# The last eight pieces of the second weights are converted beside the first transform, under new order tables

## The chip, the core and the metric

The kernel runs on one core of a Trainium2 chip. The metric is device time in microseconds (us) of that core for one execution. Three timed runs of the kernel before gave 977.62, 979.89 and 982.78 us. The profile comes from one more execution, of 984.61 us, whose span from the first to the last instruction is 982.6 us.

The core has five instruction streams. PE multiplies matrices (its weight loads are listed as PEld), DVE is the vector engine, ACT the scalar engine, POOL the GpSimd engine, and SP issues all transfers, those that transpose 16-bit data too.

## The reference

Two stages follow each other, for 4 sequences of 768 tokens.

Attention has 8 heads of width 64. Each query and key is assigned to the nearest of 16 centroids, and a query sees only keys of its own cluster:

```
mask   = q_assign[:, :, :, None] == k_assign[:, :, None, :]
scores = where(mask, scale * q @ k.T, -1e9)
out    = softmax(scores) @ v
```

The heads are laid side by side (width 512), and a feed-forward layer with a Fourier mix follows:

```
X  = fft(fft(x, axis=1), axis=2)
u  = x + real(X)
un = (u - mean(u)) / sqrt(var(u) + 1e-6)
y  = u + relu(un @ w_ch1) @ w_ch2        # w_ch1 512x2048, w_ch2 2048x512
```

All is float32. The kernel reaches that precision with pairs of float16 numbers, a high and a low part, and three products for each multiplication.

## The kernel before

The work is cut into streams that are written as generators. A plan (`Overlap.PLAN`, a string) says in which order their steps are traced; a second set of tables (`Order.TABLE`, one string for each engine) then lists the order in which each engine's instructions stand. Nothing is decided at run time: every engine works through its own list, and waits by semaphore where an operand or a buffer is not ready. The streams are:

- `p0` to `p15`, preparation of a pair of heads (four pairs to a sequence): load q and k, find the largest value (L395), scale and split into high and low (L413 on ACT, L414 on DVE), assign clusters (L446 to L481).
- `s0` to `s15`, scores: for each of six blocks of 128 queries 12 matmuls for both heads of the pair (L509) and 4 for the mask (L514), one pass on DVE for each head that finds the row's limit (L528), the exponential on ACT (L530), high and low part of it (L542 on ACT or L540 on POOL, L543 on POOL), and a transposing transfer (L545).
- `u1`, `u3`: for some early heads the transposition is done on PE instead (L562).
- `a0` to `a15`, products with v (18 matmuls for a block and head, L595 to L597, or 6 in float32, L590) and the division (L605 to L609), which writes into `X`, one 128x6x512 tile for a sequence; two such tiles take turns.
- `l` and `w`, loads and conversion of the weights. The 32 pieces (128x512 float32 each, 16 of either matrix) lie in an arena of 48 KB for each partition. `signs` takes the top bits (L698, L699 on ACT), `block` finds the largest over a group of pieces by 16 matmuls at L710 and a reduction (L714) with four tiny operations (L58 to L63), `join` rebuilds the number in PSUM (L725 on PE, L728 on DVE), `halve` writes the high part (L734 on ACT) and the low part (L740 on DVE for even pieces; L737 on ACT and L738 on POOL for odd ones). `relative` (L778 to L782) needs all pieces.
- `t0` to `t3`, the transform of a sequence: tables are loaded into the arena (L898), `fold` adds and subtracts mirrored rows and columns on DVE (L856, L857), splits (L839, L840) and transposes by transfer (L863), then come matmuls (L917, L933), three thirds with tables of their own (L906), and the sums into `X` (L983 to L992).
- `n0` to `n3`, the normalisation of the three blocks of a sequence (L1026 to L1054); the normalised rows are transposed by transfer (L1040).
- `f0` to `f3`, the two matrix products of a sequence: 576 matmuls up (L1069) and 288 down (L1111), with evictions at L1074 to L1078 and L1115.

The weights and the transform share the arena. Pieces take turns at four places (`EARLY`, at byte 0, 8224, 20576 and 28800, two pieces of 4112 bytes at each); the sign bits lie at 16448, 37024 and 41120, and a float32 copy at 45216 (`X32`). The transform's tables and folds begin at byte 20576, so with `LATE = 0` they overlap places that the weights use until the last piece is done. The class already knows a second layout for the last `2 * LATE` pieces: `place` puts them at `SPARE` (byte 0 and 8224), their sign bits at 16448, and the float32 copy over the piece itself, all below byte 20576; they are grouped by two instead of four.

PSUM has three buffers for everything but scores and outputs (`ps_f`): weights, transforms, preparation and the feed-forward products take turns in them.

Of the kernel before, what the change touches and what calls it, by code (L numbers as in the profile page):

```python
# [90 lines left out]
.2 -8 .2 9 -5 4 0 -6 5 .2 -8 0 7 -2 1 .4 3 -4 0 3 -4 1 1 .4 2 0 -4 3 .3 -7 6 .14 3 0 -5 4 .2 2 .2 -12 11 1 5 0 -21 11 1 .2 7
0 -20 10 8 -9 8 0 -6 5 -23 23 -2 1 0 -13 12 .3 -16 16 1 -4 1 1 0 2 1 4 0 -11 0 1 1 2 4 -3 -6 7 0 -4 3 0 -11 10 .4 2 -3 0 6 -6
.3 2 .2 -5 4 .2 1 -2 1 .12 7 0 -9 11 -12 12 -2 -12 0 11 -12 0 13 -14 13 -12 11 0 -13 0 4 .2 4 .3 6 0 -8 7 0 -5 4 0 -11 10 .2
13 -14 0 -15 14 .2 9 0 -11 -18 17 .3 -21 20 .2 3 3 1 -6 5 0 -7 6 .6 -13 12 .3 -15 14 .9 1 .2 6 -11 3 .2 4 0 -5 0 -3 5 0 3 1 1
# [1144 lines left out]
```

## Time and profile before

| | |
|---|---|
| timed runs | 977.62, 979.89, 982.78 us |
| profiled execution | 984.61 us, span 982.6 us |
| mean granted clock of PE | 0.984 of full speed |
| busy, of the span | PE 93%, DVE 60%, ACT 59%, POOL 59% |
| first conversion of a high half (L734) | 34.9 us |
| last one | 189.6 us |
| first matmul up (L1069) | 238.8 us |
| start of the last sequence's products, which then stand alone | 853.70 us |

Read the page's second part, 40 slices, for the stretches: PE is busy for 70 to 90% of most slices in the first quarter of the span, and for 90% or more of nearly every slice behind it, while DVE is busy for 80 to 90% of most slices of that first quarter. A share over the whole span hides both.

### The profile page before, as it was taken

What the parts mean: (1) busy time and instruction counts of PE and PEld (TensorE: products, weight loads), DVE (VectorE), ACT (ScalarE), POOL (GpSimd) and SP (SyncE); (2) the same over time, 40 slices, a digit from 0 to 9 for tenths busy, and PEclk for the clock granted to TensorE, in tenths of its full rate; (3) what the DMA queues carried; (4) which work ended last, traced back from release to release, by engine and by line L of the source; (5) the groups of instructions that cost most, each with busy time, mean ns of one, the idle gap of its engine ahead of it and who ended that gap; (6) DMA issues with size and microseconds to landing.
All of it is one profiled execution on the core that took longest, in us unless ns stands there. A gap on an engine that the chain in (4) does not pass through costs nothing.

```text
span 982.6 us, 23428 instructions
## 1 busy us (share of the span) xinstructions
PE 910.7 (93%) x9352; PEld 610.6 (62%) x9369; DVE 587.4 (60%) x1334; ACT 579.2 (59%) x924; POOL 577.7 (59%) x691
## 2 busy tenths in 40 slices
PE   2779979778999999999999999999999999999998
PEld 0347747645747657576757667567567485676583
DVE  6889899888656565678654655786463334511010
ACT  6687789557737747548756466568475472433140
POOL 2681862557967746748975658469766472553140
PEclk9989999979999999999999999999999999999999
DMA  7995894589868697598994768797684663311000
GB/s 268 200 263 138 204 258 111 125 149 184 140 146 148 110 172 149 112 180 165 138 192 89 145 122 155 137 184 142 112 135 81 121 122 65 74 24 34 11 12 22
DMA packets 359741, 131.21 MB, mean 134 GB/s; under 512 B 344272, under 2 KB 345296, under 8 KB 359632
## 3 DMA queue, kind: packets, MB, share of 16 engines
q1 hardware_dynamic: 359632, 129.72, 65.9%
q8 instruction: 73, 1.20, 0.5%
q14 instruction: 36, 0.29, 0.1%
HBM read 43.17 MB, written 6.29 MB: 50 GB/s over the span
## 4 chain that ended last, share of the span: by engine, by line
PE 46%; DMA 17%; DVE 11%; ACT 10%; POOL 8%; issue 5%; SPq 2%; POOLq 0%; ACTq 0%; DVEq 0%
PE ps_f L1069 15%; PE ps_f L1111 15%; DMA pt<-ph 14%; PE ps_big L509 5%; POOL ph L543 4%; ACT ph L542 3%; PE ps_o L590 2%; PE ps_f L917 2%; PE ps_f L562 2%; DVE arena L856 2%; ACT p L530 1%; DVE ps_big L528 1%; DVE amx L395 1%; PE ps_big L514 1%; POOL arena L1078 1%
## 5 line engine op out<-in xcount | busy, mean ns | idle before, releaser
L543 POOL TENSOR_TENSOR ph<-p,ph 128x768 f16<-128x768 f32 x144 | 241.9, 1682 | 148.1 <-ACT ph L542 120.9
L1069 PE MATMUL ps_f<-arena,w1h 128*128 128x256 f16 x1536 | 266.2, 274 | 4.8 <-DVE ps_big L528 2.3
L1111 PE MATMUL ps_f<-w2h,arena 128*128 128x512 f16 x768 | 236.8, 380 | 0.0
L1069 PE MATMUL ps_f<-arena,w1l 128*128 128x256 f16 x768 | 210.3, 274 | 0.0
L528 DVE TENSOR_SCALAR_CACHE_REDUCE ps_big<-ps_big,sce 128x768 f32<-128x768 f32 x144 | 142.5, 1021 | 91.6 <-PE ps_big L514 85.2
L1111 PEld LDWEIGHTS <-arena 128*128 128x128 f16 x1152 | 110.3, 98 | 127.5 <-issue 2.7
L530 ACT ACTIVATE p<-ps_big,rmx 128x768 f32<-128x768 f32 x144 | 129.3, 898 | 86.5 <-DVE ps_big L528 61.7
L1078 POOL TENSOR_TENSOR arena<-arena 128x256 f16<-128x256 f32 x192 | 130.3, 687 | 74.9 <-ACT arena L1077 71.6
L1069 PEld LDWEIGHTS <-w1h 128*128 128x128 f16 x1536 | 150.5, 98 | 26.1 <-issue 5.6
L542 ACT CAST ph<-p 128x768 f16<-128x768 f32 x144 | 119.8, 832 | 67.4 <-DMA pt<-ph 65.8
L1111 PE MATMUL ps_f<-w2l,arena 128*128 128x512 f16 x384 | 145.7, 379 | 0.0
L509 PE MATMUL ps_big<-hlk,hlq 64*128 64x384 f16 x1152 | 117.8, 333 | 8.3 <-ACT p L530 6.3
L595 PE MATMUL ps_o<-v,pt 128*128 128x66 f16 x1008 | 104.5, 194 | 17.9 <-DMA pt<-ph 17.4
L1074 DVE TENSOR_SCALAR arena<-ps_f,wrel 128x256 f32<-128x256 f32 x96 | 46.2, 481 | 118.0 <-PE ps_f L1069 79.3
L1077 ACT ACTIVATE arena<-ps_f,wrel 128x256 f16<-128x256 f32 x192 | 88.6, 473 | 44.3 <-DVE arena L1074 44.2
L595 PEld LDWEIGHTS <-pt 128*128 128x128 f16 x1008 | 92.6, 97 | 30.2 <-DMA pt<-ph 21.8
L596 PE MATMUL ps_o<-v,pt 128*128 128x64 f16 x1008 | 104.3, 195 | 0.0
L597 PE MATMUL ps_o<-v,pt 128*128 128x66 f16 x1008 | 103.9, 193 | 0.0
L596 PEld LDWEIGHTS <-pt 128*128 128x128 f16 x1008 | 92.9, 97 | 2.6
L597 PEld LDWEIGHTS <-pt 128*128 128x128 f16 x1008 | 93.2, 99 | 0.0
L509 PEld LDWEIGHTS <-hlq 64*128 64x128 f16 x1152 | 51.2, 96 | 59.1 <-issue 32.4
L1069 PEld LDWEIGHTS <-w1l 128*128 128x128 f16 x768 | 75.3, 98 | 11.5 <-issue 2.5
(187 smaller groups left out, 1356.7 us busy)
## 6 DMA issues: line engine op xcount, KB each, us to landing
arena<-in_moe_w_ch_dram SPq DMA_DIRECT2D x32, 512.0 KB, 5.2
scr<-in_q_dram SPq DMA_DIRECT2D x16, 384.0 KB, 3.8
vst<-in_v_dram SPq DMA_DIRECT2D x16, 384.0 KB, 4.0
scr<-in_k_dram SPq DMA_DIRECT2D x16, 384.0 KB, 4.4
out_dram<-arena SPq DMA_DIRECT2D x24, 256.0 KB, 2.3
pt<-ph SPq DMA_TRANSPOSE x156, 3.9
arena<-in_cs_dram SPq DMA_DIRECT2D x12, 192.0 KB, 4.4
arena<-in_ss_dram SPq DMA_DIRECT2D x12, 192.0 KB, 4.3
```

Of the source, the lines that this page charges most:

```text
L509: nc.tensor.matmul(out=ps[j][:, hf, 0:SH], lhsT=hq[rows[j], a, sl], rhs=hk[rows[j], c, hs], start=(i == 0), stop=False)
L528: nc.vector.tensor_scalar(out=ju, in0=ps[j][:, :, 0:SH], scalar1=ne, scalar2=None, op0=ALU.mult, op1=ALU.min, accum_out=m)
L530: nc.scalar.activation(x, ju, AF.Exp, bias=m, scale=-1.0)
L542: nc.scalar.copy(out=ph[:, 0], in_=p32)
L543: nc.gpsimd.tensor_tensor(out=ph[:, 1], in0=p32, in1=ph[:, 0], op=ALU.subtract)
L595: nc.tensor.matmul(out=o[:, at:at + W], lhsT=hi, rhs=v16[:, kt, 0:W], start=(kt == 0), stop=False)
L596: nc.tensor.matmul(out=o[:, at:at + D], lhsT=hi, rhs=v16[:, kt, 66:130], start=False, stop=False)
L597: nc.tensor.matmul(out=o[:, at:at + W], lhsT=lo, rhs=v16[:, kt, 0:W], start=False, stop=(kt == ST - 1))
L1069: nc.tensor.matmul(out=ps.rearrange("p (t x) -> p t x", x=P), lhsT=a[:, dc, fs], rhs=c[:, :, dc], start=(i == 0), stop=(i == 11))
L1077: nc.scalar.activation(hh[:, f], ps, AF.Relu, scale=rel[:, f:f + 1])
L1078: nc.gpsimd.tensor_tensor(out=hl[:, f], in0=r, in1=hh[:, f], op=ALU.subtract)
L1111: nc.tensor.matmul(out=ps, lhsT=a[:, f, ts], rhs=c[:, f], start=(i == 0), stop=(i == 47))
```

## The change

`LATE` goes from 0 to 4, so the last eight pieces of `w_ch2` (pieces 24 to 31) use the second layout, and their four groups have two pieces each: ten groups in all, not eight. The plan and the order tables are replaced as a whole.

```diff
     ID, TOP, MX, ONE = 47360, 47872, 47936, 48064
-    LATE = 0
+    LATE = 4
...
     PLAN = """
-p0 v0 c p0*2 p1 p0 p1 p0*2 c l p0*5 p1 w p2 l*3 p0 p2 l*3 w*2 p1 v1 p1*4 s0*3 w p2 w*4 p1*2 w*2 s0*2 p1 v2 w v3 s0*6 w*2 p2*2
+v0 c w p0*8 l v0 l*2 w p1*3 c p0*3 v0 p0 p2 p1 l*2 s0*2 v1 s0 a0 p1*4 w*4 v2 w*2 p1 w s0 w*2 a0 l*3 p1*2 l*3 s0 w*2 a0*2 w*2
...
     TABLE = {
         "PE": """
-.6 2 -3 2 0 -4 3 .2 1 -2 42 -39 0 -5 4 46 0 -53 4 47 -48 47 -54 7 0 -4 3 43 -44 0 -6 5 0 40 0 -41 -2 1 0 38 -39 39 -39 -2 1 0
+.5 3 0 -5 4 0 -6 5 .2 1 0 -11 12 -6 5 0 1 -7 10 0 -12 3 2 -2 1 4 -5 4 -3 2 3 -4 5 -6 0 1 0 9 -9 8 -9 8 -9 8 -9 .3 13 -14 4 0
...
```

In the kernel after, the lines that follow the tables have numbers larger by two (L856 is L858 there); the text uses the numbers of before, and only the rows below show the others.

DVE, around the first transform's fold (L856), before: the last two joins of the weights (L728) stand ahead of the fold, the last low half (L740) behind it.

```order
L609 TENSOR_TENSOR X_63<-ps_o,rs 128x3x128
L728 SCALAR_TENSOR_TENSOR ps_f<-arena,ps_f 128x512 x2
L856 TENSOR_TENSOR arena<-X_63 128x1536
L740 SCALAR_TENSOR_TENSOR w2l<-ps_f,wsc,w2h 128x512
L460 TENSOR_REDUCE mx<-ps_f 128x24
L528 TENSOR_SCALAR ps_big,rmx<-ps_big,sce 128x2x384
L462 TENSOR_TENSOR ac<-ps_f,mx 128x384
L528 TENSOR_SCALAR ps_big,rmx<-ps_big,sce 128x2x384
L395 TENSOR_REDUCE amx<-scr 128x1 x2
L395 TENSOR_REDUCE amx<-vst 128x1
L840 SCALAR_TENSOR_TENSOR arena<-arena,vseq 128x768
```

The same place after (`winv` and `wsc` are the scales of a group of pieces, `X_63` the tile of the first sequence).

```order
L611 TENSOR_TENSOR X_63<-ps_o,rs 128x3x128
L730 SCALAR_TENSOR_TENSOR ps_f<-arena,ps_f 128x512
L858 TENSOR_TENSOR arena<-X_63 128x1536
L742 SCALAR_TENSOR_TENSOR w2l<-ps_f,wsc,w2h 128x512
L397 TENSOR_REDUCE amx<-scr 128x1
L530 TENSOR_SCALAR ps_big,rmx<-ps_big,sce 128x2x384 x2
L842 SCALAR_TENSOR_TENSOR arena<-arena,vseq 128x768
L716 TENSOR_REDUCE arena<-ps_f 128x1
L858 TENSOR_TENSOR arena<-X_63 128x1536
L58 TENSOR_SCALAR ps_f<-arena 128x1
L397 TENSOR_REDUCE amx<-scr 128x1
L859 TENSOR_TENSOR arena<-arena 128x3x255
```

The fold now stands behind the first of the late groups, and the other three groups (each with a reduction like L716 and its tiny operations) stand between the transform's own instructions.

POOL at the same place before: two low halves of softmax rows (L543) and one of the weights (L738) stand ahead of the transform's second fold step (L857), which needs the fold.

```order
L543 TENSOR_TENSOR ph<-p_2706,ph 128x768
L868 TENSOR_TENSOR arena<-arena,X_63 1x255
L543 TENSOR_TENSOR ph<-p_2744,ph 128x768
L738 TENSOR_TENSOR w2l<-arena,w2h 128x512
L857 TENSOR_TENSOR arena<-arena 128x3x255
```

After, the same stretch:

```order
L483 COPY oh<-oh 128x12x16
L481 TENSOR_SCALAR oh<-oh 128x12x16
L368 MEMSET v_2975 128x6x2
L870 TENSOR_TENSOR arena<-arena,X_63 1x255
L859 TENSOR_TENSOR arena<-arena 128x3x255
L740 TENSOR_TENSOR w2l<-arena,w2h 128x512
L545 TENSOR_TENSOR ph<-p_2446,ph 128x768
L545 TENSOR_TENSOR ph<-p_2455,ph 128x768
```

The low halves now stand behind the second fold step.

POOL ahead of the first normalisation's subtraction (L1039), which the first matmul up needs, before: one softmax low half (L543) stands in the last six rows.

```order
L991 TENSOR_TENSOR X_63<-X_63,arena 128x257
L543 TENSOR_TENSOR ph<-p_3033,ph 128x768
L1048 TENSOR_TENSOR rest<-mv,mhalf 128x2
L992 TENSOR_TENSOR X_63<-X_63,arena 128x255
L1049 TENSOR_TENSOR rt<-rest 128x2
L1039 TENSOR_TENSOR arena<-arena 128x512
```

After:

```order
L740 TENSOR_TENSOR w2l<-arena,w2h 128x512
L993 TENSOR_TENSOR X_63<-X_63,arena 128x257
L994 TENSOR_TENSOR X_63<-X_63,arena 128x255
L545 TENSOR_TENSOR ph<-p_3031,ph 128x768
L1050 TENSOR_TENSOR rest<-mv,mhalf 128x2
L545 TENSOR_TENSOR ph<-p_3074,ph 128x768
L1041 TENSOR_TENSOR arena<-arena 128x512
```

The subtraction now stands behind two low halves, and behind the first two sums of the transform's last third.

Counted over the lists, these stand ahead of the first matmul up on PE: 32 blocks of scores before, 30 after; three products of 18 matmuls fewer; all weights and the whole first transform in both. On DVE, ahead of its first eviction of that product (L1074), there are 64 passes of L528 before and 60 after, 14 of L414 and 12, 8 groups of L714 with L58 to L63 and 10. After the last product of attention and ahead of the last transform's first matmul, PE has 48 matmuls of L1111 before, and 180 of L1069 and 60 of L1111 after.

## Rows read from the trace of the kernel before

**Rows 1.** The page's first part: busy us (share of the span) xinstructions.

```profile
PE 910.7 (93%) x9352; PEld 610.6 (62%) x9369; DVE 587.4 (60%) x1334; ACT 579.2 (59%) x924; POOL 577.7 (59%) x691
```

**Rows 2.** Busy time of each engine in three stretches of the span.

```profile
core 0: us, PE busy (x) PEld busy (x) DVE busy (x) ACT busy (x) POOL busy (x), PEclk, DMA share, GB/s
189.60:238.75 49.15, 32.93 (x404) 22.35 (x401) 41.65 (x90) 30.21 (x49) 29.05 (x30) 0.86 0.84 152
...
28.00:189.60 161.60, 141.22 (x1510) 96.44 (x1527) 144.55 (x325) 127.13 (x175) 92.69 (x94) 0.96 0.81 189
...
238.75:853.70 614.95, 602.58 (x6546) 404.06 (x6547) 362.63 (x815) 369.27 (x603) 406.50 (x459) 1.00 0.73 135
```

**Rows 3.** The chain of waits near its end: start us, us, what.

```profile
816.28 10.37 PE ps_f L1111 x48
...
853.70 20.96 PE ps_f L1069 x192
...
958.02 20.73 PE ps_f L1111 x96
```

**Rows 4.** One line each: counts, duration ns min/median/max, first and last start.

```profile
L734 ACT ACTIVATE w2h<-ps_f,wsc x16: 671/680/697, 127.0 to 189.6; 128x512 f16<-128x512 f32 x16
```

**Rows 5.** Groups of DVE from 189.6 to 238.75: busy, mean ns, idle before.

```profile
L856 DVE TENSOR_TENSOR arena<-X 128x1536 f32<-128x1536 f32 x2 | 7.7, 3870 | 0.0
L840 DVE SCALAR_TENSOR_TENSOR arena<-ps_f,arena 128x257 f16<-128x257 f32 (+1 forms) x7 | 2.8, 420 | 3.2 <-ACT arena L839 3.1
...
L984 DVE SCALAR_TENSOR_TENSOR arena<-ps_f,vseq,arena 128x257 f32<-128x257 f32 x2 | 1.0, 486 | 3.2 <-ACT arena L983 2.6 <-PE ps_f L917 0.6
```

**Rows 6.** Groups of DVE over the whole span.

```profile
L528 DVE TENSOR_SCALAR_CACHE_REDUCE ps_big<-ps_big,sce 128x768 f32<-128x768 f32 x144 | 142.5, 1021 | 91.6 <-PE ps_big L514 85.2 <-ACT arena L1077 4.2 <-ACT ph L542 1.6
...
L728 DVE SCALAR_TENSOR_TENSOR ps_f<-arena,ps_f 128x512 uint32<-128x512 uint32 x32 | 21.5, 689 | 0.4 <-ACT pt L567 0.4
L414 DVE SCALAR_TENSOR_TENSOR hlq<-scr,scp,hlq 128x768 f16<-128x768 f32 x16 | 20.7, 1293 | 5.0 <-ACT hlq L413 4.7
...
L740 DVE SCALAR_TENSOR_TENSOR w2l<-ps_f,wsc,w2h 128x512 f16<-128x512 f32 x8 | 6.0, 745 | 1.2 <-ACT w2h L734 1.2
...
L714 DVE TENSOR_REDUCE arena<-ps_f 128x1 f32<-128x512 f32 x8 | 5.5, 687 | 1.8 <-PE ps_f L710 1.3 <-remote 0.5
...
L58 DVE TENSOR_SCALAR ps_f<-arena 128x1 int32<-128x1 int32 x8 | 1.3, 159 | 0.1
```

**Rows 7.** The chain of waits from 160 us: one block of scores.

```profile
160.12 1.08 PE ps_big L509 x12
161.21 0.27 PE ps_big L514 x4
```

**Rows 8.** Timeline of PE: the first matmul of a product, and the one behind it.

```profile
573.44 0.20 PE L595 MATMUL ps_o<-v,pt 128*128 128x66 f16 x1
...
574.00 0.38 PE L1111 MATMUL ps_f<-w2h,arena 128*128 128x512 f16 x1
```

**Rows 9.** Timeline of POOL from 188.3 us.

```profile
188.82 0.72 POOL L868 TENSOR_TENSOR arena<-arena,X 1x255 f32<-1x255 f32 x1
189.51 1.63 POOL L543 TENSOR_TENSOR ph<-p,ph 128x768 f16<-128x768 f32 x1
191.11 1.14 POOL L738 TENSOR_TENSOR w2l<-arena,w2h 128x512 f16<-128x512 f32 x1
```

**Rows 10.** Timeline of DVE: the first fold, and a later one.

```profile
188.86 5.01 DVE L856 TENSOR_TENSOR arena<-X 128x1536 f32<-128x1536 f32 x1
...
412.28 1.76 DVE L856 TENSOR_TENSOR arena<-X 128x1536 f32<-128x1536 f32 x1
```

**Rows 11.** PE's queue at L1069: a wait in the queue, as in rows 4.

```profile
L1069 PEldq EVENT_SEMAPHORE  x7: 51/51/3172, 235.5 to 933.0; - x7
```

**Rows 12.** Groups of POOL over the whole span.

```profile
L543 POOL TENSOR_TENSOR ph<-p,ph 128x768 f16<-128x768 f32 x144 | 241.9, 1682 | 148.1 <-ACT ph L542 120.9 <-ACT arena L983 6.0 <-DVE ac L462 5.1
...
L738 POOL TENSOR_TENSOR w2l<-arena,w2h 128x512 f16<-128x512 f32 x8 | 9.3, 1158 | 15.8 <-ACT arena L737 13.3 <-DMA arena<-in_sd_dram 2.5
```

More of the change, by code (lines that the diff above doesn't have):

```diff
@@ L91 @@
[L91 to L94, printed above, removed]
@@ new lines @@
+-23 49 -60 0 14 -14 0 12 .2 109 -110 .2 -18 0 16 .2 1 .3 1 2 -3 2 -3 2 .4 116 0 -94 -10 -16 15 11 -28 12 10 -8 10 -11 10 -5
+-7 23 -24 23 -24 23 -24 3 3 0 7 -8 0 2 3 -4 0 -5 0 5 0 5 .7 1 -2 -10 10 -13 31 9 -30 0 3 46 -47 47 -48 .4 -10 0 8 17 -18 0 3
+-15 10 5 .3 -9 0 7 5 .6 7 -3 -24 5 22 -3 -20 12 9 22 -37 38 -39 35 -36 12 -12 1 10 2 -13 1 14 0 -6 0 -11 10 3 1 -6 39 0 -35
+34 0 -40 1 1 0 56 .2 -59 0 2 1 .2 42 1 -45 .5 1 -2 1 6 -7 24 -25 5 18 -25 5 8 -15 5 8 -15 5 8 -9 8 15 -16 .2 -8 27 -40 51 -30
@@ L123 @@
+6 -7 6 -7 6 -7 6 2 -10 6 0 12 .5 -16 15 -16 15 0 -20 19 .2 10 5 -8 1 5 -6 5 -39 32 5 -6 5 -6 5 -41 .6 12 26 -27 .7 13 .4 1 .7
 """,
         "Activation": """
[L125 to L127 removed]
@@ new lines @@
+8 -9 17 -18 20 0 -20 20 2 -20 19 0 13 -28 16 -16 15 1 -18 20 -21 23 -22 1 15 9 -26 23 -6 .2 21 2 -13 -9 8 -9 8 -9 1 -2 7 -15
+7 1 -2 7 131 -135 0 8 1 -10 13 4 29 0 -50 1 8 -9 1 6 -6 1 19 -20 19 -17 .3 3 -2 1 3 .2 2 1 -15 12 4 -15 10 1 -2 2 0 20 -21
+-17 0 42 60 -61 61 -62 61 -62 61 -61 -33 0 18 -12 21 1 -12 -2 -20 0 11 -12 0 10 .2 -13 16 -14 13 .2 7 .2 -26 25 -26 28 0 6
+-37 0 35 -13 .2 10 1 43 -16 -40 0 12 1 -15 12 -13 .2 45 -43 9 -9 8 0 -10 9 -10 9 .2 -9 8 -9 8 1 -2 1 .2 19 2 21 -45 1 -2 1 .2
@@ L166 @@
+0 27 -28 0 19 -20 1 .6 3 .6 1 10 -11 .2 2 5 .15 2 -3 2 -3 2 .3
 """,
@@ new lines @@
+f0*2 v8 f0 t1*2 f0 t1 p9 s8 f0 p10 f0 a8*2 s8 f0 s8 f0 p10 t1*4 p10 t1 p11 p10 t1 p10 t1*8 p12 t1 n1 p9*2 n1 f0 p10 v10 t1*3
+f0*2 p10 t1 p11 v10 f1*2 s9 f1*2 s9 v12 f1 a8 s9 v13 f1 a8*11 s9 f1 p10*2 f1 s9*2 p11 v9 p11 s9 f1*2 s9 v9 s9 f1 n1 s9*3 f1
+p10 f1 n1 p10 f1*2 p11 f1 p10 s10 f1 p11*2 s10*4 f1 p11 f1 s10 a9 p11 a9 f1 a9*2 s10 f1 t1 p11 a9 s10*3 f1 a9 p12 s10 a9*5
+s10 a9*2 f1 a9 f1*4 p12 f1 p12*2 n1 p11 f1 p11 f1*3 n1 f1 p12*2 f1 a10*4 f1 a10 f1 s11*2 a10*5 v11 a10 f1 a10*2 f1 a10 s11*6
@@ new lines @@
+f1*4 v11 p12*2 a11 s11 p13 a11 v12 s11*3 f1 p12*3 f1 p13 a11 p13 a11*4 s12 f1 a11 f1 a11 f1 s12 p13 f1*5 a11 f1*4 p14 p13 f1
+p13 s12 p13 f1 s12 f1*2 a11*2 p13 a11*2 p13 f1 s12 f1 p13 f1*2 v12 s12*5 f1 p14 f1 t2 f1*2 t2 f1 v13 t2*4 v15 p14*2 t2*6 v14
+t2*2 p14 p15 t2*2 p15 s12 t2*6 a12 p14 f1 p13 a12 f1 n2 f1 f2 p15 t2 f2 p14 f2 p13 p14*2 p15 f2*2 a12 p14 t2 a12 f2 a12 s12
+f2 p15 a12 v13 f2*6 a12*2 f2 a12*2 p15 a12*4 p14 s13 f2*2 s13 f2 s13*2 f2 a13*3 s13*4 v14 p15*3 v14 s13*3 a13*4 p15 s13 f2
@@ L1154 @@
+a13*3 p14 a13*2 s14 p15 a13 s14 a14 a13 n2 s14*3 p15 s14*5 a14 s14*2 a14*3 v15 n2 a14 f2 a14 f2*2 a14 s15 a14*3 f2 a14 s15*2
+a14 s15 a14 s15 n2 s15*2 a15 f2 s15*2 f2 s15 f2 s15 f2 n2 f2 s15 t3 f2 n2 f2*6 v15 a15*8 f2 a15*5 f2*28 t3 f2*5 t3*14 f2 t3*3
+n3 t3 n3 t3 f2 t3 f2 f3 t3*2 f3*18 n3 f3*19 n3 f3 n3 f3*13 n3 f3*20
 """
```

159 lines of the change are left out of this document (72 added, 87 removed).

## Prediction

> **What bounds the kernel now.** I began with the busy shares [rows 1]: PE 93%, the others near 60%. A share over the span says nothing on stretches with different limits, so the second view was the busy time by stretch [rows 2]. From 238.75 us, where the first matmul up stands, to 853.70 us PE is busy 602.58 of 614.95 us, 98%; the chain of waits shows what follows: only the last sequence's products, 20.96 and 20.72 us in turn, to 958.02 + 20.73 = 978.75 us [rows 3]. Nothing can be won there but 12.4 us of idle PE. Ahead of the first matmul up it is different. From 28.00 to 189.60 us DVE is busy 144.55 of 161.60 us (89%), PE 141.22 at a granted clock of 0.96; from 189.60 us, the start of the last high half of a weight piece [rows 4], to 238.75 us DVE is busy 41.65 of 49.15 us (85%) and PE 32.93 us at 0.86. So the time has two parts: up to the first matmul up DVE paces, behind it PE does, and what PE has not done by then it must do later. A change gains only if it brings the first matmul up forward by more than the PE work that it pushes behind it.
>
> The third view was DVE's own groups in the 49.15 us [rows 5]. Idle is 49.15 - 41.65 = 7.5 us, of which 3.1 us wait for ACT's high halves of the transform (ahead of L840) and 2.6 us for L983: 5.7 us in which the transform's chain PE, ACT, DVE stands without other work. And the two folds took 7.7 us, although one of them alone takes 1.76 us [rows 10].
>
> **The change, part by part.** All times are taken off the profiled execution, 984.61 us, span 982.6 us; it lies 4.7 us above the median of 979.89 us, and the sum is moved by that much at the end.
>
> *What is taken from the first part, and comes back in the second.* On DVE four passes of L528 go (4 x 1.021 = 4.1 us) and two of L414 (2 x 1.293 = 2.6 us); two groups of the weights come, each with one L714 (0.687 us) and four operations of the size of L58 (4 x 0.159 = 0.64 us), so 2 x 1.33 = 2.7 us [rows 6]. One division and one set of scales less, two batch statistics more: I count these as nothing. DVE is 4.0 us shorter, and since it paces there, the first matmul up comes 4.0 us sooner. PE, however, has two blocks of scores fewer ahead of it (2 x (1.08 + 0.27) = 2.7 us [rows 7]) and three products (3 x (574.00 - 573.44) = 1.7 us [rows 8]): 4.4 us that stand in the PE-bound part now. Together +0.4 us. This exchange is a wash, which is the main thing to see about it.
>
> *The folds.* The first fold takes 5.01 us [rows 10], and meanwhile POOL runs L868, a softmax low half and a weight's low half without a gap, to 192.25 us [rows 9]; where it stands alone it takes 1.76 us. POOL's operations hold DVE's back. In the new list only L868's like (0.72 us) and some small ones stand ahead of the second fold step on POOL, and the low halves behind it. So I put the first fold at 1.76 + 0.72 = 2.5 us, 5.01 - 2.5 = 2.5 us saved on the pacing engine. From both sides: it saves at most 5.01 - 1.76 = 3.3 us; and if POOL arrives late with earlier low halves, it costs as much as now and saves nothing. The second fold has two low halves beside it in both kernels; taken as no change.
>
> The Trainium skill, "SBUF — State Buffer", section "Who interferes with whom", calls the port pair that DVE and GpSimd share an exclusive lock: whoever starts first holds it for the whole instruction. The 5.01 us against 1.76 us agree, since the fold ran on only after POOL's last operation had ended. By that rule the four late low halves on POOL, now among the transform's two-input operations, can also block DVE, each by its whole length; with 1.16 us for each of them the sum would be 4.6 us worse, and about nothing would be left of the gain.
>
> *The waits inside the transform.* Three whole late groups and the rest of the first now stand between the transform's instructions on DVE. They are work that DVE did ahead of the transform before, and can fill the 5.7 us [rows 5]. But the four L840 of the even part still stand in a row with nothing between them, as before. Bounds: all 5.7 us filled; or none, and the new waits for PE's and ACT's part of a group add as much again, +5.7. I take a bit over half, 3.0 us saved, since three of the seven L840 and the L984 have other work ahead of them in the list.
>
> *The first matmul up itself.* Before, PE's queue stood 3.17 us at it [rows 11]. On POOL the subtraction that it needs now stands behind two low halves of 1.682 us where one stood [rows 12], and behind two sums of the last third. That is +1.7 us on this chain, if it sets the start. But it does so only if it ends behind DVE's work, and DVE has more between the last third and its first eviction than before. Bounds 0 and +3.4 us; I take 0.
>
> *The rest of the list.* The order is new everywhere, also where no weight is left. Behind the first matmul up the work is the same; all that can change is 12.4 us of PE's idle time [rows 2]. I take 0, bounds -6 and +6. At the end 180 matmuls up and 60 down now cover the last fold (by the dense 20.96/192 and 20.73/96 us each, 32.6 us), where 48 took 10.37 us [rows 3]; but fewer stand between the transform's matmuls. PE lost little there before; 0.
>
> Sum: +0.4 - 2.5 - 3.0 = -5.1 us. 984.61 - 5.1 = 979.5 us for an execution like the profiled one, and 979.89 - 5.1 = 974.8 us for the median.
>
> **The rivals.**
>
> *More than that: the whole first part is denser.* DVE's idle time from 28.00 to 238.75 us is 17.05 + 7.5 = 24.5 us [rows 2]. A transform that may start before the weights end gives a longer stretch to sort in. With half of the idle gone, and the folds as above, -12.2 - 2.5 + 0.4 = -14.3 us: 965.6 us. Against it: 17.05 of the 24.5 us lie where no transform stands in either kernel.
>
> *No change.* The folds find POOL in their way again, and the waits inside the transform stay, each on another group: +0.4 us, 980.3 us. For it speaks that DVE's 85 to 89% is high for an engine whose every other instruction depends on another engine.
>
> *Slower: the late groups come into the transform's chain.* All four have the same serial steps: reduction and four tiny operations 1.33 us, join 0.689, high half on ACT 0.680 [rows 4], low half 0.745 [rows 6], 3.4 us in all. They take the same three PSUM buffers as the transform. If a transform step waits for a buffer that a piece holds, and the piece waits for DVE behind another wait of the transform, the two chains add up instead of hiding each other: 4 x 3.4 = 13.8 us at most, half of it 6.9 us; with none of the gains 979.9 + 6.9 = 986.8 us. It decides from the point where DVE's waits for ACT and PE between the fold and the first matmul up are over 5.7 us in sum. Against it: the lists put most of a group's steps some rows apart.
>
> *That the change doesn't do what it says* I leave out as a case: the lists show the late groups beside the transform.
>
> **How the numbers follow.** The forecast (970 to 980 us) has 0.42, the denser first part 0.20, no change 0.17, the slower case 0.21. A measurement of this kernel can tell about 0.5%, 4.9 us, from no change, so faster means below 975.0 us and slower above 984.8. Of the forecast I count 0.25 as faster and 0.17 as within. Faster 0.25 + 0.20 = 0.45; within 0.17 + 0.16 = 0.33; slower 0.22, with 0.01 from the no-change case. The range for 8 in 10 is 963 to 987 us: it takes in the denser case and the slower one up to its half price; the forecast alone with its bounds is 968 to 982.
>
> **What would show it.** The first matmul up should stand at about 238.75 - 4.0 - 2.5 - 3.0 = 229 us; at 235 us or later the gain is gone, at 245 us the slower case holds. The first fold should last 2.5 us, not 5; if it takes 5 us that term is wrong. DVE's waits at L840 and L984 for the first transform should be near 2.7 us. From the first matmul up to the last the time should be 4.4 us longer than now, 740.0 us (238.75 to 978.75), with PE busy at 98% of the middle part. What would make it wrong as a whole: a middle part with over 18 us of idle PE, or one whose idle time falls by half, for which I have no row.

## The result, and the profile after

The changed kernel takes 992.07 us (median of 4 runs, 989.68 to 993.29) against 978.75 us (977.31 to 982.78) of the kernel before: ratio 1.0113 [1.0082, 1.0144], slower by 1.1%. 974.8 us were predicted, in a range that ended at 987.

The profiled execution after took 992.49 us (span 990.7), close to its median. The one of before that the prediction rests on, 984.61 us, was above its median; a second profile of the same kernel (run e0 below, 979.03 us, span 977.1) lies on it, and is the partner here. Single profiles of one order differ by some microseconds, so where it matters the range over several is given too. The busy shares, against [rows 1], say nothing:

```profile
PE 917.5 (93%) x9369; PEld 613.5 (62%) x9369; DVE 579.4 (58%) x1344; ACT 583.9 (59%) x924; POOL 578.6 (58%) x691
```

The stretches say nearly all, as in [rows 2]: up to the first matmul up, from there to the dense products of the last sequence, and the rest. First the kernel before (e0), then after.

```profile
core 0: us, PE busy (x) PEld busy (x) DVE busy (x) ACT busy (x) POOL busy (x), PEclk, DMA share, GB/s
28.00:236.50 208.50, 169.37 (x1911) 117.13 (x1925) 186.35 (x417) 157.51 (x222) 122.53 (x123) 0.97 0.82 181
236.50:848.20 611.70, 602.37 (x6546) 403.93 (x6547) 361.86 (x811) 369.40 (x603) 406.70 (x459) 1.00 0.73 136
```

```profile
28.00:236.50 208.50, 175.84 (x1838) 117.94 (x1837) 176.50 (x405) 149.69 (x209) 114.87 (x112) 0.91 0.77 175
236.50:861.80 625.30, 607.49 (x6640) 407.56 (x6638) 364.42 (x831) 382.13 (x616) 414.84 (x469) 1.00 0.72 135
```

Both first matmuls up start at 236.5 us, although DVE has 9.85 us less to do ahead of it (186.35 - 176.50) and PE 73 matmuls fewer. Nor is this an accident of the pair: the six profiled kernels with before's order up to there (before, e0, e2, e3, e10, e16; e3 and e10 change a few places in it) have it at 236.5 to 238.8 us, the three with after's (after, e6, e9) at 236.5 to 240.8. With the fewer matmuls PE is busy 6.5 us longer in that stretch, at a granted clock of 0.91 instead of 0.97.

Ahead of the first fold (L856, L858 after) alone, e0 and then after:

```profile
28.00:185.88 157.88, 135.59 (x1500) 94.29 (x1514) 143.28 (x324) 126.07 (x172) 92.03 (x93) 0.99 0.82 190
```

```profile
28.00:183.15 155.15, 135.51 (x1438) 93.26 (x1438) 131.67 (x297) 110.30 (x151) 82.80 (x86) 0.95 0.75 177
```

DVE has 11.6 us less to do there, and the fold starts 2.7 us sooner; the other 8.9 us have become idle time of DVE (23.5 us against 14.6). PE is as busy as before, with 62 matmuls fewer.

The middle part is 13.6 us longer: 5.1 us more work for PE (607.49 - 602.37), and 8.5 us more idle PE (17.8 against 9.3; the first profile of before has 12.4, so 5.5 against that one). The end is the same; the chain of waits of after (start us, us, what) answers [rows 3] row for row:

```profile
805.02 19.65 PE ps_f L1071 x180
824.67 12.95 PE ps_f L1113 x60
...
861.80 20.96 PE ps_f L1071 x192
...
966.12 20.73 PE ps_f L1113 x96
```

128.9 us lie behind the start of the dense products in both kernels. So the 13.6 us between the two spans are 0 + 5.1 + 8.5 + 0.

In the transform itself, the timeline of DVE and POOL of after (start us, us, engine line op) shows the first fold at 1.97 us, where [rows 10] had 5.01, and the second fold step L859 ahead of the low half L740, where [rows 9] had the low halves first:

```profile
182.79 0.72 POOL L870 TENSOR_TENSOR arena<-arena,X 1x255 f32<-1x255 f32 x1 [2.94 <-DVE X L611]
183.15 1.97 DVE L858 TENSOR_TENSOR arena<-X 128x1536 f32<-128x1536 f32 x1
185.20 1.81 POOL L859 TENSOR_TENSOR arena<-arena 128x765 f32<-128x765 f32 x1 [1.70 <-DVE arena L858]
186.97 1.16 POOL L740 TENSOR_TENSOR w2l<-arena,w2h 128x512 f16<-128x512 f32 x1
```

DVE's groups from the fold to the first matmul up (183.2 to 236.5 us; busy, mean ns, idle before) against [rows 5]: the two folds have shrunk from 7.7 to 3.7 us, as the term on them said. The waits at the two lines were 3.2 + 3.2 us [rows 5] and 2.9 + 3.2 us in e0, and are 3.7 + 2.0 us after. Of these ACT ended 5.7, 5.5 and 4.0 us; for 1.7 us of after the profile shows no releaser.

```profile
L840 DVE SCALAR_TENSOR_TENSOR arena<-ps_f,arena 128x257 f16<-128x257 f32 (+1 forms) x7 | 2.8, 421 | 2.9 <-ACT arena L839 2.9
...
L984 DVE SCALAR_TENSOR_TENSOR arena<-ps_f,vseq,arena 128x257 f32<-128x257 f32 x3 | 1.4, 470 | 3.2 <-ACT arena L983 2.6 <-PE ps_f L917 0.5
```

```profile
L858 DVE TENSOR_TENSOR arena<-X 128x1536 f32<-128x1536 f32 x2 | 3.7, 1855 | 0.0
L842 DVE SCALAR_TENSOR_TENSOR arena<-ps_f,arena 128x257 f16<-128x257 f32 (+1 forms) x7 | 2.8, 421 | 3.7 <-ACT arena L841 3.7
...
L986 DVE SCALAR_TENSOR_TENSOR arena<-ps_f,vseq,arena 128x257 f32<-128x257 f32 x3 | 1.5, 487 | 2.0 <-issue 1.7 <-ACT arena L985 0.3
```

All idle time of DVE from the fold to the first matmul up is 8.5 us after, and 7.5 in e0 and in the first profile.

And one saved stretch came back elsewhere. The fold starts at 183.2 us, 2.7 us sooner than in e0, and is 3 us shorter; the first matmul up comes 53.4 us behind its start, not 50.6. Set off from the fold's start (e0 against after): first transform matmul 17.6 and 11.4 us, last of the seven L840 (now L842) 25.0 and 23.0, second L1036 of the normalisation (now L1038) 41.3 and 45.0. A lead of 6 us is lost on the way and turns into a lag of 4. Among the profiles of before's order 50.6 us is the longest way, 48.1 the shortest; the three of after's have 53.4 to 53.6.

### The profile page after: what moved, and what is told of

Its sections match the earlier page's. It is cut to its first block, busy times and chain, and to the rows that moved or that the text cites. A ratio compares the mean times of both kernels' runs of the same rounds, so it can differ in the third digit from the quotient of the medians.

```text
span 990.7 us, 23443 instructions
## 1 busy us (share of the span) xinstructions
PE 917.5 (93%) x9369; PEld 613.5 (62%) x9369; DVE 579.4 (58%) x1344; ACT 583.9 (59%) x924; POOL 578.6 (58%) x691
## 4 chain that ended last, share of the span: by engine, by line
PE 60%; DMA 16%; POOL 9%; ACT 5%; DVE 4%; issue 4%; SPq 1%; POOLq 0%; ACTq 0%; DVEq 0%
PE ps_f L1113 20%; PE ps_f L1071 19%; DMA pt<-ph 14%; PE ps_big L511 6%; POOL ph L545 5%; PE ps_f L919 3%; PE ps_o L592 2%; ACT ph L544 2%; PE ps_o L597 2%; PE ps_big L516 1%; PE ps_o L598 1%; PE ps_o L599 1%; PE ps_f L564 1%; POOL p L545 1%; SPq L547 1%
## 5 line engine op out<-in xcount | busy, mean ns | idle before, releaser
L545 POOL TENSOR_TENSOR ph<-p,ph 128x768 f16<-128x768 f32 x144 | 246.0, 1711 | 144.7 <-ACT ph L544 137.8
L544 ACT CAST ph<-p 128x768 f16<-128x768 f32 x144 | 119.7, 832 | 89.0 <-DMA pt<-ph 88.4
L511 PE MATMUL ps_big<-hlk,hlq 64*128 64x384 f16 x1152 | 121.2, 335 | 9.7 <-ACT p L532 5.0
L597 PE MATMUL ps_o<-v,pt 128*128 128x66 f16 x1008 | 107.4, 195 | 17.9 <-DMA pt<-ph 13.8
L1079 ACT ACTIVATE arena<-ps_f,wrel 128x256 f16<-128x256 f32 x192 | 89.7, 475 | 47.5 <-DVE arena L1076 46.8
L598 PE MATMUL ps_o<-v,pt 128*128 128x64 f16 x1008 | 107.1, 196 | 0.0
L599 PE MATMUL ps_o<-v,pt 128*128 128x66 f16 x1008 | 106.6, 194 | 0.0
L511 PEld LDWEIGHTS <-hlq 64*128 64x128 f16 x1152 | 53.3, 96 | 62.5 <-issue 35.1
```

The costliest lines, as they stand in the source:

```text
L511: nc.tensor.matmul(out=ps[j][:, hf, 0:SH], lhsT=hq[rows[j], a, sl], rhs=hk[rows[j], c, hs], start=(i == 0), stop=False)
L544: nc.scalar.copy(out=ph[:, 0], in_=p32)
L545: nc.gpsimd.tensor_tensor(out=ph[:, 1], in0=p32, in1=ph[:, 0], op=ALU.subtract)
L597: nc.tensor.matmul(out=o[:, at:at + W], lhsT=hi, rhs=v16[:, kt, 0:W], start=(kt == 0), stop=False)
L598: nc.tensor.matmul(out=o[:, at:at + D], lhsT=hi, rhs=v16[:, kt, 66:130], start=False, stop=False)
L599: nc.tensor.matmul(out=o[:, at:at + W], lhsT=lo, rhs=v16[:, kt, 0:W], start=False, stop=(kt == ST - 1))
```

## The experiments

Line numbers are those of before for kernels built on it, and 2 higher for kernels built on after; e1 and e2 have numbers 16 lower than before. Every ratio is against the kernel before.

**e0: the kernel before, profiled once more.**

> The kernel before, unchanged, for a second profile: the profiled execution of before was 4.7 us longer than the median of its timed runs. If that was an accident of the one execution, this profile has a span of about 977 us, and the 4 to 6 us are missing at one or a few places; where, decides which of the rows of before can be compared with the kernel after. If instead a profiled execution is always longer, the span is 982 us again. Timed against before: ratio 1.000 within 0.003.

978.75 us, 0.9994 [0.9979, 1.0009]. The two profiles (spans 982.6 and 977.1 us) differ by 2.3 us up to the first matmul up and by 3.2 in the middle part. The granted clock, 0.984 and 0.991, does not explain it alone: e10 has a span of 977.9 us at 0.984.

**e1 and e2: which half of the order costs?** e1 has after's order up to the first matmul up and before's behind it; e2 the other way round, and with the layout of before:

```
-    LATE = 4
+    LATE = 0
```

> LATE = 4 and the order of the kernel after on every engine up to its first matmul up; from there everything that is left stands in the order of the kernel before. Theory A (the loss of 13 us lies mostly in the new order behind the first matmul up): the first matmul up at about 236.5 us as in after, idle PE in the middle part back near the 12.4 us of before, time 981 to 984 us (4.4 us of moved PE work less 2.2 us that the first part gained). Theory B (the first part is the loss: late groups in the transform's chain, more half-speed clock): 988 to 992 us. Theory C (what counts is the seam, the two parts were sorted for each other): 984 to 988 us here and in the next kernel both.

999.26 us, 1.0192 [1.0169, 1.0215]. As a test of the first part it failed: the seam made a chain of its own, which the stretch before its first matmul up shows (PE busy 12.70 of 18.80 us at a clock of 0.59). Behind the seam before's order runs as in before, with 12.3 us of idle PE.

```profile
236.50:255.30 18.80, 12.70 (x134) 7.04 (x132) 10.06 (x32) 11.22 (x15) 12.06 (x15) 0.59 0.70 128
255.30:867.80 612.50, 600.21 (x6545) 403.58 (x6546) 360.32 (x812) 369.60 (x603) 403.67 (x457) 1.00 0.72 135
```

> LATE = 0 and the order of the kernel before on every engine up to its first matmul up; from there everything that is left stands in the order of the kernel after. Theory A: idle PE of 17 to 18 us in the middle part, time 984 to 988 us. Theory B: 978 to 981 us, as before. Theory C: 984 to 988 us.

986.18 us, 1.006 [1.0039, 1.0081]: 5.9 us more, with no late piece in the kernel and the first matmul up at 238.1 us. The middle part has before's PE work, 601.70 us, and after's idle time, 17.3 us.

```profile
238.10:857.10 619.00, 601.70 (x6545) 404.12 (x6544) 358.58 (x813) 373.59 (x606) 409.70 (x461) 1.00 0.71 134
```

So the idle PE of the middle belongs to the order behind the first matmul up: it comes with that order without a late piece, and goes with before's (e1).

**e3: the fold freed, alone.** In before, on POOL:

```order
 L868 TENSOR_TENSOR arena<-arena,X_63 1x255
+L857 TENSOR_TENSOR arena<-arena 128x3x255
 L543 TENSOR_TENSOR ph<-p_2744,ph 128x768
 L738 TENSOR_TENSOR w2l<-arena,w2h 128x512
-L857 TENSOR_TENSOR arena<-arena 128x3x255
```

> The kernel before with one change in POOL's list: the first transform's second fold step (L857) stands right behind L868 and ahead of one softmax low half (L543) and one low half of the weights (L738). If POOL's operations hold the fold back, the first fold (L856) lasts 1.8 to 2.5 us, not 5.0. If DVE paces up to the first matmul up, as the prediction says, that matmul and the end come 2.5 us sooner: 976.2 us against 978.7. Rival: the fold is shorter, but DVE waits that much longer for ACT and PE behind it (L840, L984), and the time stays at 978.7 within 1 us. Slower by 1 to 2 us if the two low halves, now later, hold the next product.

980.47 us, 1.0006 [0.999, 1.0023]: nothing. The timeline shows that the edit took: the fold lasts 1.75 us, and L857 starts 2.3 us behind its start, not 5.

```profile
188.12 1.75 DVE L856 TENSOR_TENSOR arena<-X 128x1536 f32<-128x1536 f32 x1
188.14 2.31 POOL L868 TENSOR_TENSOR arena<-arena,X 1x255 f32<-1x255 f32 x1
190.42 1.80 POOL L857 TENSOR_TENSOR arena<-arena 128x765 f32<-128x765 f32 x1
```

The first matmul up still comes 48.8 us behind the fold, where e10 below, whose L857 starts 5.0 us behind it, has 49.3. Part of what the folds gain is lost again on DVE: the two folds take 4.9 us in e3 where e0 has 7.8, but two later operations 3.5 where e0 has 2.0:

```profile
L840 DVE SCALAR_TENSOR_TENSOR arena<-arena,vseq 128x768 f16<-128x768 f32 x2 | 3.5, 1740 | 0.0
```

And before itself does not always have the long fold: with POOL's list of before it takes 5.0 us in before and e0, 2.9 in e5, and 1.75 in e2, e4, e10 and e16. So timed runs of before may have the short fold too, and e3's ratio tests less than the whole 2.5 us. The first matmul up shows no gain either: 236.5 and 238.8 us with the long fold, 236.9 to 238.5 with the short one (e2, e3, e10, e16).

**e4, e5, e10: who paces the first part?** Work is added to before: e4 gives DVE 12 reductions of 0.95 us more (pairs 2 to 5), e5 gives PE 12 blocks' scores a second time (pairs 2 and 3), e10 gives DVE 8 passes of 0.93 us inside the first transform (`more`, one reduction each), ahead of the L840 and L984 that wait (one of the two places is shown).

```
e4
-        self.nc.vector.tensor_reduce(out=m[:, i:i + 1], in_=x, op=ALU.max, axis=AX.X, apply_absolute_value=True)
+        for _ in range(2 if pr in (2, 3, 4, 5) else 1): self.nc.vector.tensor_reduce(out=m[:, i:i + 1], in_=x, op=ALU.max, axis=AX.X, apply_absolute_value=True)
e5
-        for hf in range(2):
+        for n, hf in enumerate((0, 1, 0, 1) if pr in (2, 3) else (0, 1)):
e10
-            nc.scalar.activation(am, pa[:, 0:NL], AF.Copy, scale=iy)
+            nc.scalar.activation(am, pa[:, 0:NL], AF.Copy, scale=iy); self.more(b == 0 and t < 2)
```

> The kernel before, and each of the largest-value passes (L395) of pairs 2 to 5 is done twice: 12 more passes of 0.95 us, 11.4 us of DVE work between 34 and 161 us, which change no number. Theory P, the prediction's premise (DVE paces up to the first matmul up): that matmul stands 11 us later, at about 248 us, and the whole takes 990 us. Theory Q (no engine paces there; the time is one chain of waits that goes through every engine): DVE has 48 of the 211 us of the chain that ends at the first matmul up, a quarter, so the first matmul up comes 0 to 4 us later and the whole takes 979 to 983 us.

> The kernel before, and for the 12 score blocks of pairs 2 and 3 the 12 matmuls of L509 are done twice: 12 x 1.08 = 13.0 us of PE work between 94 and 167 us, which change no number. Theory P (DVE paces): PE has 39 us of idle time there and hides it, the whole stays at 979 to 981 us. Theory Q (a chain through every engine, PE with 43% of it): the first matmul up comes 4 to 8 us later, the whole takes 983 to 987 us. If PE alone paced, 13 us: 992 us.

> The kernel before, and DVE makes eight more passes of about 0.95 us (a largest value over 768 numbers, into a word that nothing reads), 7.6 us in all: one ahead of each of six L840 and two L984 of the first transform, the places where DVE waited 5.7 us for ACT. The prediction took it that work put there fills the waits: then the way from the fold to the first matmul up grows by 2 us at most (it is 47.5 to 50.6 us), and the whole takes 979 to 981 us. Theory G (each single wait is about 0.46 us, shorter than any instruction that is put there, so the chain grows by what does not fit): 3 us. Theory A (the chain's waits are for what DVE itself has to deliver; everything adds): 7.6 us, 986 to 987 us.

e4: 986.29 us, 1.0074 [1.0052, 1.0096], +7.2 us (by the ratio) for 11.4 us of DVE. e5: 995.36 us, 1.0174 [1.0145, 1.0202], +17 us for 13.0 us of PE. e10: 980.17 us, 1.0012 [0.9996, 1.0029], nothing for 7.5 us. These are whole times, the middle part included. The first matmul up stands at 246.8 us in e4 and 247.3 in e5, 8.1 to 10.8 us later than in e0 and the first profile of before, for either engine's extra work:

```profile
28.00:246.84 218.84, 182.95 (x1929) 121.89 (x1928) 193.36 (x426) 158.76 (x222) 124.11 (x123) 0.91 0.78 174
```

```profile
28.00:247.25 219.25, 188.04 (x2072) 127.16 (x2072) 185.94 (x412) 158.67 (x220) 122.40 (x123) 0.93 0.79 173
```

So e4 came out near what theory P said of that place (248 us), and e5 did not (no change). In e10 the passes fill the waits exactly as the prediction wanted them filled by late pieces (DVE's groups from the fold to the first matmul up; L840 waits 0.4 us, L984 0.6, against 3.2 and 3.2 in [rows 5]):

```profile
L843 DVE TENSOR_REDUCE junk<-ident 128x1 f32<-128x768 f32 x8 | 7.5, 932 | 0.0
...
L840 DVE SCALAR_TENSOR_TENSOR arena<-ps_f,arena 128x257 f16<-128x257 f32 (+1 forms) x7 | 2.8, 410 | 0.4 <-ACT arena L839 0.4
...
L984 DVE SCALAR_TENSOR_TENSOR arena<-ps_f,vseq,arena 128x257 f32<-128x257 f32 x2 | 1.0, 476 | 0.6 <-ACT arena L983 0.6
```

The first matmul up stands 49.3 us behind the fold, as in before. The waits have room for work that needs no other engine; that late pieces are such work it does not show.

**e8, e11, e14: the normalisation behind the late pieces.** e8 is after with the first block's normalisation moved forward in the lists of all engines: on ACT ahead of a softmax (shown), the subtractions on DVE and POOL and the transfers likewise, and on PE the first 24 matmuls up ahead of two products and a block of scores. e11 adds another place for the second half of the normalised rows, and e14 has that place alone.

```order
 L1040 CAST arena<-arena 128x512
+L1038 ACTIVATE arena<-X_63,rpow 128x512
+L1040 CAST arena<-arena 128x512
 L532 ACTIVATE p_3074<-ps_big,rmx 128x768
 L544 CAST ph<-p_3074 128x768
-L1038 ACTIVATE arena<-X_63,rpow 128x512
-L1040 CAST arena<-arena 128x512
```

```
e11, e14
-            un = at(self.UN[j], [P, DM], F32)
+            un = at(0 if j and b == blk == 0 else self.UN[j], [P, DM], F32)
```

> The kernel after, with the first block's normalisation and the first two matmul groups up moved forward in the lists and nothing else: on ACT L1038 and L1040 of the second half ahead of an exponential (L532) and a high half, on POOL its subtraction (L1041) ahead of two low halves (L545), on DVE the first half's subtraction ahead of the last late group's reduction, the two transposing transfers (L1042) ahead of the softmax's, and on PE the first 24 matmuls up ahead of two products and a block of scores. Theory N (the first matmul up is late because its own chain, from the sums of the transform on, stands behind softmax and late-group work: 13.1 us from the sums to the second L1038 in after, 7.5 in before): the first matmul up comes 4 to 5 us sooner against the fold, 48 to 49 us behind it where it was 53.4 to 54.2, and the whole takes 988 to 990 us. Rival: the first matmul up is sooner, but the products and scores that it passes come later by the same time, and the total stays at 991 to 993 us.

> The kernel of the run with the normalisation moved forward, and one buffer placed elsewhere: the first block's second half of normalised rows (L1038, 2 KB a partition) lies at byte 0 of the arena, where piece 28 was, instead of byte 16384. There it shared bytes with the sign bits of the late groups (16448 to 20544), and in both runs so far L1038 began in the moment in which the last late join (L730) ended: 228.3 us in after, 233.2 in the run with the moved list. Theory B (these shared bytes put the late groups on the chain to the first matmul up): L1038 of the second half begins within 1.5 us of its own operand, 225 to 231 us, the first matmul up stands 47 to 49 us behind the fold instead of 52 to 54, and the whole takes 988 to 992 us, 7 to 10 us less than the run with the list alone (998.9). Rival: something else holds it, first matmul up and time as in that run, 997 to 1001 us.

> The kernel after with its own lists, and only that buffer at byte 0. In ACT's list an exponential and a high half, which ended at 228.3 us, stand ahead of the second L1038, so its start can hardly move: theory B gains 0 to 1.5 us here, 990 to 992 us. If the list had been held up elsewhere by ACT's wait for the join, 3 us or more are gained: below 989 us.

e8: 998.88 us, 1.0187 [1.0162, 1.0212]. e11: 1000.23 us, 1.0188 [1.0158, 1.0218]. e14: 993.92 us, 1.0136 [1.0099, 1.0174]. In after and in e8 the second L1038 starts when the last join of a late piece (L730) has ended, 0.03 us behind it. In after that decides nothing, since ACT's own L544 ends at the same time, 228.24:

```profile
227.41 0.83 ACT L544 CAST ph<-p 128x768 f16<-128x768 f32 x1
227.50 0.69 DVE L730 SCALAR_TENSOR_TENSOR ps_f<-arena,ps_f 128x512 uint32<-128x512 uint32 x1
228.22 0.81 ACT L1038 ACTIVATE arena<-X,rpow 128x512 f32<-128x512 f32 x1
```

In e8 ACT stands for 3.34 us, and its own operand had been there for 4 us (L1036 at 228.91):

```profile
228.91 0.20 DVE L1036 TENSOR_SCALAR rpow<-mv,rpow 128x1 f32<-128x1 f32 x1
232.39 0.68 DVE L730 SCALAR_TENSOR_TENSOR ps_f<-arena,ps_f 128x512 uint32<-128x512 uint32 x1
233.10 0.81 ACT L1038 ACTIVATE arena<-X,rpow 128x512 f32<-128x512 f32 x1 [3.34 <-DVE ps_f L730]
```

With the buffer elsewhere (e11) it starts behind its own operand and ahead of the joins:

```profile
228.31 0.20 DVE L1036 TENSOR_SCALAR rpow<-mv,rpow 128x1 f32<-128x1 f32 x1
229.08 0.81 ACT L1038 ACTIVATE arena<-X,rpow 128x512 f32<-128x512 f32 x1
231.80 0.68 DVE L730 SCALAR_TENSOR_TENSOR ps_f<-arena,ps_f 128x512 uint32<-128x512 uint32 x1
```

L1038 and the join have no number in common: the buffer lies at bytes 16384 to 18432, and the late pieces' sign bits begin at 16448. That is a dependency of bytes, and in e8 it makes the normalisation wait for the last late piece. Its price is small: from e8 to e11 the way from the fold to the first matmul up goes from 52.1 to 50.9 us, and the time does not fall. With after's own lists (e14) it is not seen at all: the second L1038 still starts behind L544, and that way is 54.3 us, where after has 53.4.

```profile
228.68 0.83 ACT L544 CAST ph<-p 128x768 f16<-128x768 f32 x1
229.41 0.81 ACT L1038 ACTIVATE arena<-X,rpow 128x512 f32<-128x512 f32 x1
```

In e11 the first matmul up waits 2.91 us for a PSUM buffer of the last piece instead (L742). What makes e8 and e11 slower than after stands behind the first matmul up: the block of scores and the two products that their lists push there (PE is busy 613.19 us in the middle of e11), and more idle PE (20.6 us).

**e7: the softmax high halves off POOL.** In after, the 24 that POOL makes go to ACT.

```
-    PC = (0, 1, 2, 3, 4, 5)
+    PC = ()
```

> The kernel after, with one change: the 24 high halves of the first pairs' softmax that POOL copied (L542, 0.82 to 0.89 us each) are copied by ACT (L544, 0.83 us), at the same places. The chain that ends at the first matmul up in the kernel after has 43 us of POOL (36 of them the low and high halves of the softmax) and 46 us of the transposing transfers behind them, where before's has none of POOL and 12 us of these transfers. Theory R (the first part of the kernel after is paced by the softmax through POOL): POOL is relieved of 20 us, and the first matmul up comes 4 to 9 us sooner, the whole takes 983 to 988 us. Rival: ACT's list is in order and full enough; each copy now stands behind other work there, and the first matmul up stays or comes up to 4 us later, 991 to 996 us.

994.17 us, 1.0144 [1.012, 1.0168]; first matmul up at 240.5 us, 54.2 behind the fold, no sooner. Relieving POOL at ACT's cost gains nothing there; ahead of the fold POOL is busy 64 instead of 83 us, ACT 127 instead of 110.

**e6, e9, e16: the products and their transfers.** In e6 the products of after stand later in PE's list, in e9 ACT's and POOL's softmax steps stand sooner, and in e16 the products of before are moved sooner, by up to 6 us (order tables only).

> The kernel after, and only PE's list behind the first matmul up is changed, with the divisions of DVE that belong to it: each product (18 matmuls, L597 to L599) that began less than 7 us behind the issue of its transposing transfer (L547) is moved back in the list to 7 us behind it, where the buffers allow. Theory S (the new order puts products too close behind their transfers: 39 of 134 begin within 6 us of the issue, 15 or 16 of 131 in the order of before; a transfer takes 3.8 us, and PE waits 16.7 us for them against 6.3): the waits of L597 for these transfers fall to 6 us, PE's idle time in the middle part from 17.8 to about 12 us, and the time to 986 to 988 us. Rival: PE meets other waits in their place (evictions, scores, the transform), and the time stays at 990 to 993 us.

> The kernel after, and behind its first matmul up the work of the softmax (L532, L544 on ACT, L545 on POOL, the transfers L547) stands up to 2 us further forward in the lists, never ahead of what it needs: 535 instructions by 1.6 us on average. PE's list is unchanged. Theory S (PE loses 6 us more in the middle part than before because the products stand too close behind the softmax): PE's waits for the transfers fall from 16.7 us to about 10, the whole takes 987 to 990 us. Rival, from the run with later products, where the waits moved to scores and evictions: what the softmax gains, the evictions on the same engines lose, and the time is 991 to 995 us.

> The kernel before, and only PE's list behind the first matmul up is changed: products stand up to 6 us further forward, not less than 5 us behind the issue of their transposing transfer. By the times of before the median distance goes from 14.7 to 9.4 us and 44 instead of 15 products stand within 6 us, as in the kernel after (8.6 us, 39 within 6). Theory S (this closeness is enough to cost the middle part its 6 to 8 us): PE's waits for these transfers go from 6 to 12 us or more, idle PE there from 9 to 12 us to 16 or more, and the time to 985 to 988 us. Rival (closeness is only a sign of the other list, and PE has other work in its queue): the time stays at 978 to 981 us.

The rows are groups of PE in the middle part (busy, mean ns, idle before and releasers): before (e0), after, e6, e16.

```profile
L595 PE MATMUL ps_o<-v,pt 128*128 128x66 f16 x792 | 80.8, 193 | 2.3 <-DMA pt<-ph 2.3
L509 PE MATMUL ps_big<-hlk,hlq 64*128 64x384 f16 x768 | 75.7, 324 | 1.6 <-ACT p L530 1.4
```

```profile
L597 PE MATMUL ps_o<-v,pt 128*128 128x66 f16 x811 | 84.1, 193 | 7.8 <-DMA pt<-ph 6.7 <-DVE X L611 0.9
L511 PE MATMUL ps_big<-hlk,hlq 64*128 64x384 f16 x792 | 78.6, 324 | 3.2 <-ACT p L532 3.1
```

```profile
L511 PE MATMUL ps_big<-hlk,hlq 64*128 64x384 f16 x798 | 82.0, 328 | 8.1 <-ACT p L532 8.0
L597 PE MATMUL ps_o<-v,pt 128*128 128x66 f16 x816 | 86.0, 194 | 2.7 <-DVE arena L842 1.9 <-DVE X L611 0.6 <-DMA pt<-ph 0.2
```

```profile
L595 PE MATMUL ps_o<-v,pt 128*128 128x66 f16 x792 | 82.3, 193 | 9.0 <-DMA pt<-ph 5.7 <-DVE X L609 2.6 <-DVE ps_f L627 0.6
```

Of after's 8.5 us more idle PE, 5.5 stand ahead of the products' first matmuls and 1.6 ahead of scores. The transposing transfer takes as long as before (median 3.9 us, 3.8 in e0), but is issued later against its product: from its issue to the first matmul that reads it pass 14.5 us at the median in before and 8.6 in after, and 39 of 134 are closer than 6 us, where 15 to 17 of 131 were; e2, with after's order there, has 8.4 us and 39. e16 makes that distance shorter in before's own list (median 11.6 us, 28 closer than 6): 997.9 us, 1.0167 [1.0136, 1.0197], and 24.2 us of idle PE in the middle. So moving products closer costs time, but the transfers' waits are the smaller part of it: 5.7 us in e16 against 2.3 in e0 and 4.0 in the first profile, of 12 to 15 us more idle PE, and e16 loses more than after with fewer close products. Nor does distance alone give it back: e6 took the transfers' waits away (2.7 us of idle left), and ended at 999.06 us, 1.0196 [1.0167, 1.0225], with the time now ahead of scores, 8.1 us for ACT's exponential. e9 was worst, 1027.88 us, 1.0492 [1.0469, 1.0515]: ACT's exponentials went ahead of its evictions, and PE then waited 16.6 us for L1079. The exponentials and the evictions share ACT's queue, and what one gained there the other lost.

No kernel beat before.

## Why the prediction was wrong

**The exchange (+0.4) was half right.** The work that goes behind the first matmul up was put at 4.4 us and measured 5.1. The other half, "DVE is 4.0 us shorter, and since it paces there, the first matmul up comes 4.0 us sooner", failed: 9.85 us less on DVE ahead of it and 236.5 us as before. The premise failed here, "up to the first matmul up DVE paces". It was read from 85 to 89% busy. Of 11.6 us taken from DVE ahead of the fold 8.9 became idle time. e4 and e5 say why the share misled: ahead of the transform 11.4 us more on DVE put the first matmul up 8.1 to 10.4 us later, and 13.0 us more on PE 8.5 to 10.8. Both engines' work counts, so what is taken from one can turn into waits for the other, and PE's share of that stretch did not fall: 135.5 us in both, with fewer matmuls at a clock of 0.95 instead of 0.99. What ended the 8.9 us, wait by wait, was not separated.

The Trainium skill, "Perfetto Trace Analysis", section "Identifying the Most-Contended Engine", tells one to take the engine with the highest occupancy and to optimize it first. The kernel after does not bear that out for the first part: DVE is the busiest engine there [rows 2], 11.6 us less of its work ahead of the fold brought 2.7 us, and the measurement decides.

**The folds (-2.5).** The first fold became 1.97 us long, as said. But the 5.01 us that it was set against belonged to that execution more than to the list (1.75 us in e2, e4, e10 and e16, with POOL's list of before), and in e3, where it is short, the first matmul up stands at 236.9 us, where before and e0, with the long one, have 238.8 and 236.5. The step that failed is "saved on the pacing engine"; no gain is seen from the term.

**The waits inside the transform (-3.0).** They were to be near 2.7 us, and are 5.7 us at the two lines where e0 has 6.1 (the 5.7 of the prediction were ACT's share alone). e10 bears out one half, that these waits can take work at no cost; the other half failed, that late groups are such work: DVE's idle time grew by 1.0 us, and the way from the fold to the first matmul up by 2.8 us over e0 and 3.5 over the first profile. That is the direction of the slower rival, whose chains add up through what they share, but only small pieces of it are seen. A transform step does wait for a PSUM buffer that a late piece holds, but for 0.6 us (the waits of after from 190 to 209 us: engine, line, waited for; us, times, longest):

```profile
PE ps_f L881 <- DVE w2l L742: 0.6, 1, 0.6
```

The bytes that the normalised rows and the sign bits have in common, which I had not looked for, hold e8 for 3.34 us and after not at all (e14). Nor does the sum price what PE does last. In after's chain of waits ahead of the first matmul up a transposing transfer of 3.79 us leaves PE without work. The granted clock, 1.00 before, is 0.66 from 228.0 to 236.5 us, so part of that stretch is at the lower level, 1.2 GHz, and the block of scores behind the transfer takes 2.04 us where [rows 7] had 1.08:

```profile
228.17 3.79 DMA pt<-ph
...
233.17 2.04 PE ps_big L511 x12
```

How much of the 53.4 us each of these takes was not separated.

**The first matmul up itself (0)** held: from the second L1036 (L1038 after) to POOL's subtraction pass 2.2 us in e0 and in after, so the second low half on POOL did not make that way longer. By the times, the first matmul up waits for the transfer behind that subtraction: in e0 it is issued at 231.79 us, takes 4.6 us to land, and PE's queue stands 3.78 us until 236.48, like the 3.17 us of [rows 11].

```profile
L1069 PEldq EVENT_SEMAPHORE  x1: 3779/3779/3779, 232.7 to 232.7; - x1
```

In after it lands at 236.37 us, 3.4 us behind its issue, and PE, behind the scores above, is at work until the same time: two chains end there together.

**The rest of the list (0, bounds -6 and +6)** is the largest miss: 0 was taken, and it measured +8.5 against e0 and +5.5 against the first profile. "All that can change is 12.4 us of PE's idle time" was taken to bound the loss as well; idle time can be added beyond it (24.2 us in e16). e2 puts it on the order behind the first matmul up (17.3 us of idle PE), and e16 shows that another order of before's own work can cost more than that, with products closer behind their transfers. What makes this order leave 8.5 us more of PE idle, wait by wait, stays open: two attempts to remove one kind (e6, e9) moved it to another.

**The tail (0)** held: 128.9 us in both.

In sum, against e0: 0 for the -9.5 of the three gains, +5.1 for the exchange's other half, +8.5 for the list: 13.6 us. The signs named beforehand came half: the middle part with nearly 18 us of idle PE is there, but the first matmul up at 236.5 us lies past 235 ("the gain is gone") and short of 245. The slower rival's price, 986.8 us, missed the middle part's share.

## What to carry to other kernels

A high busy share does not make an engine the pacer. Before a term is counted as saved on it, add a few microseconds of work to it ahead of the place in question, and then to a second engine: where both move the end, work taken from one of them can become a wait for the other. Extra work in an engine's waits shows only that the waits have room. A duration that depends on which engine starts first needs more than one execution before a gain is counted on it. A new order is not free where the work is unchanged: look at the distance between a transfer's issue and its first reader in the new list, for every reader, and do not take the idle time that there is now for a bound of the loss. Where work is moved beside other work into shared memory, compare the byte ranges of everything alive there, not only the buffers that the change names.

## What the runs showed of the hardware

One start of a few hundredths of a microsecond decides which of DVE and POOL is held. In before L868 starts 0.04 us ahead of the fold, is done in 0.72 us, and the fold takes 5.01 [rows 9, 10]; in e3 the fold starts 0.02 us ahead, takes 1.75 us, and the same L868 takes 2.31. The Trainium skill, "SBUF — State Buffer", section "Who interferes with whom", says that issue order decides who blocks, for the whole instruction; these two runs agree. The price did not turn up in e3's time.
